# Output stores moved from ScalarE's DMA queue to SyncE's, and a small weight loaded between pieces of a larger one, in a retention and mixer kernel

## The chip, the cores and the metric

One core of one Trainium2 chip at a time. Times are microseconds (us) of device time for one execution. The profiler's span is the same execution without some 1.8 us at its start and end. A run counts as slow when it is more than 1.5% above the fastest of the same kernel, and else as fast. A ratio is the mean time of one kernel's fast runs over that of the kernel before, so it is not quite the ratio of the medians quoted; its 95% interval stands in brackets. The clock of a run is the mean share of its full clock that TensorE was granted.

## The reference, cut to what matters

```python
# q, k, v: (4 batches, 8 heads, 768 positions, 64)
state = gamma * state + k_t v_t^T ;  y_t = scale * q_t state      # retention
x = y as (4, 768, 512)
h  = x^T @ U @ V                  # U: 768 x 32, V: 32 x 768
u  = x + h^T
out = u + relu(u @ w_ch1) @ w_ch2 # 512 -> 2048 -> 512
```

The kernel calls u @ w_ch1 the up products and the second product the down products. It turns u by transposing DMAs (tile uT) before the up products of batches 2 and 3.

## The kernel before: the parts concerned

All loads are issued by SyncE (SP) in the order of a list. U and V go as one entry, ahead of w1:

```python
if key[0] == "uv":
    nc.sync.dma_start(out=Uf..., in_=moe_U...)
    for c in range(NCB):                       # NCB = 4
        nc.sync.dma_start(out=Vf[ds(RK * c, RK)], in_=moe_V)
    return
...
feed.append((("uv",), None))
for mb in range(4):
    for c in range(NCB):
        feed.append((("w1", mb, c), moe_w_ch1[ts(c, P), ts(mb, 512)]))
...
def prep_w1(mb):                               # GpSimd casts w1
    for c in range(NCB):
        nc.gpsimd.tensor_copy(out=w1b[:, c, ts(mb, 512)], in_=take("w1", mb, c))
        feed_one()                             # and the next load is issued
...
def hold_v():                                  # ScalarE casts V
    nc.scalar.activation(V4, Vf, AF.Copy)
```

A finished row block of the output (128 x 512, 256 KB) is put on a list of stores, with the engine that will issue it, and the turn of u is three transposing DMAs, of two row blocks each:

```python
def lr_turn(b, j):                             # j = 0 and 2; the third call is j = 4
    nc.sync.dma_start_transpose(
        out=uTs[b][:, ds(j, 2)]..., in_=us[b][:, ds(j, 2)]...)
...
elif r[1] == 2:
    stores.append((nc.sync if b > 1 else nc.scalar, out[b, ts(j, P)], r[0]))
```

So batch 1's six stores are issued by ScalarE, in the same microseconds in which SP issues batch 2's transposes.

Of the kernel before, what the change touches and what calls it, by code (L numbers as in the profile page):

```python
# [18 lines left out]
def kernel(  # L19
# [11 lines left out]
    nc = tc.nc  # L31
# [73 lines left out]
    feed = []  # L105
# [3 lines left out]
    def pair(b, sc):  # L109
        i = 2 * sc  # L110
        qs = [("q", b, sc, hh) for hh in range(2)]
        if b == 1:
            return [("k", b, i), *qs, ("v", b, i), ("k", b, i + 1),
                    ("v", b, i + 1)]
        return [("k", b, i), ("k", b, i + 1), *qs, ("v", b, i),
                ("v", b, i + 1)]

    def feed_keys(keys):
        for nm, b, i, *hh in keys:
            if nm == "q":  # L120
                src = q[b, ds(4 * hh[0], 4), ts(i, SC), :].rearrange(
                    "h (p two) d -> p h (two d)", two=2)
            else:
                src = (k if nm == "k" else v)[b, :, ts(i, P), :].rearrange(
                    "h p d -> p h d")
            feed.append(((nm, b, i, *hh), src))
# [8 lines left out]
    def feed_one(hold=True):  # L135
        if n_fed[0] == len(feed):
            return
        if hold and feed[n_fed[0]][0][:2] == ("k", 3):
            return
        key, src = feed[n_fed[0]]  # L140
        n_fed[0] += 1
        if key[0] == "uv":
            nc.sync.dma_start(
                out=Uf.rearrange("p s two r -> p s (two r)"),
                in_=moe_U.rearrange("(s p two) r -> p s (two r)", p=P, two=2))
            for c in range(NCB):
                nc.sync.dma_start(out=Vf[ds(RK * c, RK)], in_=moe_V)
            return
        t = rin.tile([P, 512], fp32, tag="in", name=f"in_{n_fed[0]}")
        ready[key] = t  # L150
        if key[0] in "qkv":
            t = t.rearrange("p (h d) -> p h d", h=H if len(key) == 3 else 4)
        nc.sync.dma_start(out=t, in_=src)  # L153

    def take(*key):
        assert feed[n_used[0]][0] == key, (feed[n_used[0]][0], key)
        n_used[0] += 1
        return ready.pop(key, None)
# [4 lines left out]
    for mb in range(4):  # L163
        for c in range(NCB):
            feed.append((("w1", mb, c), moe_w_ch1[ts(c, P), ts(mb, 512)]))
    feed_keys(pair(1, 0)[:AHEAD])
    for m in range(NM):
        feed.append((("w2", m), moe_w_ch2[ts(m, P)]))
# [3 lines left out]
    for _ in range(RING):  # L172
        feed_one()
# [79 lines left out]
    def prep_block(eng, nm, sc, hh):  # L253
        if hh == 0:
            pre[nm, sc] = blk.tile([P, 2, H, D], bf16, tag=nm + "0",
                                name=f"{nm}0_{sc}")
        t = pre[nm, sc][:, :, ds(4 * hh, 4)]
        src = take(nm, 0, sc, hh).rearrange("p (h two d) -> p two h d", h=4,
                                            two=2)
        if nm == "v":  # L260
            if eng == "A":
                nc.scalar.activation(t, src, AF.Copy)
            else:
                (nc.vector if eng == "D" else nc.gpsimd).tensor_copy(out=t,
                                                                     in_=src)
        else:
            g = (gq0 if nm == "q" else gk0)[:, sc, :, ds(4 * hh, 4), None]
            (nc.gpsimd if eng == "P" else nc.vector).tensor_tensor(
                t, src, g.to_broadcast([P, 2, 4, D]), op=ALU.mult)
        feed_one()  # L270

    def prep_keys(b, keys):
        for key in keys:
            nm, _, i, *hh = key
            src = take(*key)
            sc = i if nm == "q" else i // 2
            if nm == "q":
                if not hh[0]:
                    pre["q", b, i] = rpre.tile([P, 2, H, D], bf16, tag="qd",
                                               bufs=3, name=f"qd_{b}_{i}")  # L280
                t = pre["q", b, i][:, :, ds(4 * hh[0], 4)]
                src = src.rearrange("p (h two d) -> p two h d", h=4, two=2)
                g = gq0[:, i, :, ds(4 * hh[0], 4), None].to_broadcast(
                    [P, 2, 4, D])
            else:
                src = src.rearrange("p (h d) -> p h d", h=H)
            if nm == "k":
                if i % 2 == 0:
                    pre["k", b, sc] = rpre.tile([P, 2, H, D], bf16, tag="kd",
                                                bufs=3, name=f"kd_{b}_{sc}")  # L290
                t = pre["k", b, sc][:, i % 2]
                g = gk[:, i, :, None].to_broadcast([P, H, D])
            if nm == "v":
                t = rpre.tile([P, H, D], bf16, tag="vd", name=f"vd_{b}_{i}")
                pre["v", b, i] = t
                nc.gpsimd.tensor_copy(out=t, in_=src)  # L296
            else:
                nc.gpsimd.tensor_tensor(t, src, g, op=ALU.mult)  # L298
            feed_one()
# [23 lines left out]
    def prep_w1(mb):  # L323
        for c in range(NCB):
            nc.gpsimd.tensor_copy(out=w1b[:, c, ts(mb, 512)],  # L325
                                  in_=take("w1", mb, c))
            feed_one()

    def prep_w2(j):
        for m in range(4 * j, 4 * j + 4):  # L330
            nc.gpsimd.tensor_copy(out=w2b[:, m], in_=take("w2", m))  # L331
            feed_one()
# [3 lines left out]
    live = {}  # L336
# [245 lines left out]
             tp.rearrange("p (n t) -> p n t", t=P))  # L582

    def lr_turn(b, j):
        nc.sync.dma_start_transpose(
            out=uTs[b][:, ds(j, 2)].rearrange("p j c t -> p (j c) t"),
            in_=us[b][:, ds(j, 2)].rearrange("p j m -> p (j m)"))
# [7 lines left out]
    stores = []  # L595
# [32 lines left out]
    def down_pairs(b, gT, gS):  # L628
# [15 lines left out]
        def row(j):  # L644
            if j not in rows:
                rows[j] = [outp.tile([P, DM], fp32, tag="o_sb",
                                     name=f"o_{b}_{j}"), 0]
            return rows[j]
# [10 lines left out]
        def give(key, i, j, h, more):  # L659
            r = row(j)  # L660
            nc.vector.tensor_tensor(r[0][:, ds(DQ * h, DQ)], acc[key, i], more,
                                    op=ALU.add)
            r[1] += 1
            if end and i + 1 == NP:
                stores.append((nc.sync, out[b, ts(j, P), ds(DQ * h, DQ)],
                               r[0][:, ds(DQ * h, DQ)]))
            elif r[1] == 2:
                stores.append((nc.sync if b > 1 else nc.scalar,
                               out[b, ts(j, P)], r[0]))

        def p1(i):
# [3 lines left out]
        def p2(i):  # L675
            product("B", i, a12, w21, True)
            give("B", i, i, 0, held["a", i])
# [7 lines left out]
        def c22(i, nm):  # L685
            done.add((nm, i))
            if ("p5", i) in done and ("p7", i) in done:
                give("C", i, i + NP, 1, held["c", i])
# [32 lines left out]
        def p4(i):  # L721
            product("A", i, a22, t4, False)
            give("A", i, i + NP, 0, us[b][:, i + NP, :DQ])
# [175 lines left out]
    for mb in range(4):  # L899
        prep_w1(mb)  # L900
# [19 lines left out]
    for b in range(1, B + 1):  # L920
        tracks = []
        if b > 1:
            old = b - 1 < SEVEN
            first = [part(lr_expand, b - 1, 4, 2, "qk" if old else "st"),
                     part(lr_turn_pe, b - 1, 4, "qk" if old else "o")
                     if b < 3 else part(lr_turn, b - 1, 4)]
            if not old:
                RINGS["mlp"] = [6, 0, 1, 2]
# [131 lines left out]
```

## Time and profile before

| before | value |
|---|---|
| time, median of 3 runs | 221.32 us (221.21 to 221.44) |
| span of the profiled run | 220.5 us (its time was 222.3, 1 us above the median) |
| TensorE busy | 210.1 us |
| TensorE's wait for uT at 132.17 us | 1.95 us |

Two more lines of the page of the kernel before: the bytes of ScalarE's queue (packets, MB, share of 16 engines' span), and the costliest group of matmuls, whose last column is TensorE's idle time just before them and what ended most of it.

```profile
q10 hardware_dynamic: 1008, 1.64, 2.4%
...
L748 PE MATMUL mlp<-uT,w1b 128*128 128x512 f16 (+1 forms) x512 | 88.4, 326 | 2.5 <-DMA uT<-x 1.9
```

Of the 2.5 us that TensorE stood before all 512 up products, 1.9 are the one wait for the turned u. q10 is small over the whole span.

### The profile page before, as it was taken

What the parts mean: (1) busy time and instruction counts of PE and PEld (TensorE: products, weight loads), DVE (VectorE), ACT (ScalarE), POOL (GpSimd) and SP (SyncE); (2) the same over time, 40 slices, a digit from 0 to 9 for tenths busy, and PEclk for the clock granted to TensorE, in tenths of its full rate; (3) what the DMA queues carried; (4) which work ended last, traced back from release to release, by engine and by line L of the source; (5) the groups of instructions that cost most, each with busy time, mean ns of one, the idle gap of its engine ahead of it and who ended that gap; (6) DMA issues with size and microseconds to landing.
All of it is one profiled execution on the core that took longest, in us unless ns stands there. A gap on an engine that the chain in (4) does not pass through costs nothing.

```text
span 220.5 us, 5496 instructions
## 1 busy us (share of the span) xinstructions
PE 210.1 (95%) x2224; PEld 146.2 (66%) x2224; DVE 145.8 (66%) x300; ACT 92.9 (42%) x191; POOL 82.8 (38%) x119
## 2 busy tenths in 40 slices
PE   6879989999899999999999969999999999999994
PEld 2568744485555554656888854757788856668884
DVE  6478656233989539799686762598986443867443
ACT  3347664466446335667712005867510035551000
POOL 5466658998896869100089900000000000000000
PEclk9999999999999999999999999999999999999999
DMA  5999899999999999999999999600006340000043
GB/s 161 302 293 245 252 330 300 321 393 263 235 241 231 235 210 234 172 312 255 209 245 227 197 243 185 73 1 3 0 3 156 119 139 17 0 4 0 18 152 119
DMA packets 84569, 39.12 MB, mean 177 GB/s; under 512 B 58432, under 2 KB 77504, under 8 KB 84544
## 3 DMA queue, kind: packets, MB, share of 16 engines
q1 hardware_dynamic: 83536, 37.14, 72.0%
q10 hardware_dynamic: 1008, 1.64, 2.4%
q8 instruction: 17, 0.28, 0.6%
q14 instruction: 8, 0.07, 0.1%
HBM read 27.75 MB, written 6.29 MB: 154 GB/s over the span
## 4 chain that ended last, share of the span: by engine, by line
PE 69%; DMA 19%; DVE 3%; ACT 3%; POOL 2%; SPq 2%; issue 1%; DVEq 0%; ACTq 0%
PE mlp L748 28%; PE A L640 13%; DMA in<-in_moe_w_ch_dram 7%; PE mlp L799 7%; DMA in<-in_k_dram 6%; PE C L640 4%; DMA uT<-x 3%; PE B L640 3%; DMA in<-in_q_dram 2%; PE o L530 2%; ACT qT L85 2%; PE o L525 1%; PE s L491 1%; PE mlp L191 1%; SPq L153 1%
## 5 line engine op out<-in xcount | busy, mean ns | idle before, releaser
L748 PE MATMUL mlp<-uT,w1b 128*128 128x512 f16 (+1 forms) x512 | 88.4, 326 | 2.5 <-DMA uT<-x 1.9
L758 ACT ACTIVATE gT<-mlp 128x512 f16<-128x512 f32 (+1 forms) x98 | 47.3, 490 | 64.7 <-PE mlp L748 63.1
L748 PEld LDWEIGHTS <-w1b 128*128 128x128 f16 x512 | 48.2, 98 | 32.8 <-issue 2.1
L756 DVE TENSOR_SCALAR gT<-mlp 128x512 f16<-128x512 f32 (+1 forms) x30 | 16.6, 555 | 27.7 <-PE mlp L748 26.7
L640 PEld LDWEIGHTS <-gT 128*128 128x128 f16 x288 | 27.7, 98 | 3.3
L799 PE MATMUL mlp<-w2b,gT 128*128 128x512 f16 x96 | 23.7, 380 | 0.0
L298 POOL TENSOR_TENSOR kd<-in,gk 128x512 bf16<-128x512 f32 x18 | 19.2, 1082 | 4.6 <-DMA in<-in_k_dram 3.9
L640 PEld LDWEIGHTS <-gS 128*128 128x128 f16 x200 | 19.2, 98 | 2.6
L298 POOL TENSOR_TENSOR qd<-in,gq 128x512 bf16<-128x512 f32 x18 | 19.5, 1104 | 0.0
L640 PE MATMUL A<-w2t,gT 128*128 128x256 f16 x144 | 18.4, 273 | 0.0
L85 ACT ACTIVATE state<-st 64x256 bf16<-64x256 f32 x40 | 15.0, 374 | 6.7 <-PE st L371 3.8
L85 ACT ACTIVATE x<-o 128x512 f16<-128x512 f32 x20 | 11.9, 596 | 13.6 <-PE o L530 13.3
L501 DVE TENSOR_TENSOR a<-s,mask 128x512 bf16<-128x512 f32 x24 | 15.3, 680 | 2.4 <-PE s L491 2.4
L799 PEld LDWEIGHTS <-gT 128*128 128x128 f16 x96 | 8.4, 98 | 7.7 <-issue 0.2
L296 POOL CAST vd<-in 128x512 bf16<-128x512 f32 x18 | 11.2, 632 | 2.6 <-DMA in<-in_v_dram 2.4
L325 POOL CAST w1b<-in 128x512 f16<-128x512 f32 x16 | 9.7, 613 | 4.0 <-DMA in<-in_moe_w_ch_dram 3.4
L331 POOL CAST w2b<-in 128x512 f16<-128x512 f32 x16 | 10.0, 627 | 0.8
L640 PE MATMUL B<-w2b,gT 128*128 128x256 f16 x72 | 9.3, 273 | 0.0
L640 PE MATMUL A<-w2t,gS 128*128 128x256 f16 x72 | 9.0, 273 | 0.0
L640 PE MATMUL A<-w2b,gT 128*128 128x256 f16 x72 | 8.8, 273 | 0.0
L567 DVE TENSOR_TENSOR x<-s,x 128x256 f16<-128x256 f32 (+1 forms) x16 | 8.1, 548 | 0.6 <-PE qk L561 0.5
L593 POOL COPY gate<-gT 128x1 f16<-128x1 f16 x1 | 0.2, 190 | 21.9 <-DVE gT L593 21.9
(148 smaller groups left out, 292.2 us busy)
## 6 DMA issues: line engine op xcount, KB each, us to landing
in<-in_moe_w_ch_dram SPq DMA_DIRECT2D x32, 256.0 KB, 5.2
in<-in_k_dram SPq DMA_DIRECT2D x24, 256.0 KB, 5.5
in<-in_q_dram SPq DMA_DIRECT2D x24, 256.0 KB, 4.7
in<-in_v_dram SPq DMA_DIRECT2D x24, 256.0 KB, 5.3
out_dram<-o SPq DMA_DIRECT2D x16, 256.0 KB, 2.2
out_dram<-o ACTq DMA_DIRECT2D x6, 256.0 KB, 4.2
Vf<-in_moe_V_dram SPq DMA_DIRECT2D x4, 96.0 KB, 5.4
out_dram<-o SPq DMA_DIRECT2D x3, 128.0 KB, 1.7
```

The source lines that it names most:

```text
L85: nc.scalar.activation(dst, src, AF.Copy)
L296: nc.gpsimd.tensor_copy(out=t, in_=src)
L298: nc.gpsimd.tensor_tensor(t, src, g, op=ALU.mult)
L325: nc.gpsimd.tensor_copy(out=w1b[:, c, ts(mb, 512)], in_=take("w1", mb, c))
L331: nc.gpsimd.tensor_copy(out=w2b[:, m], in_=take("w2", m))
L501: nc.vector.tensor_tensor(a, four(sp[i]), causal(mask), op=ALU.mult)
L567: nc.vector.tensor_tensor(us[b][:, ds(j0, nj), ts(c, P)], four(grown[b][c])[:, :nj], xs[b][:, ds(j0, nj), ts(c, P)], op=ALU.add)
L640: nc.tensor.matmul(acc[key, i], lhs[:, m, ts(i, P)], rhs[:, m], start=(fresh and m == 0), stop=(m == NH - 1), skip_group_check=True)
L748: nc.tensor.matmul(g_p[:, :sz], w1b[:, c, ts(m, P)], uTs[b][:, ds(j, nj), c], start=(c == 0), stop=(c == NCB - 1))
L756: nc.vector.tensor_relu(gT[:, m, ds(lo, sz)], g_p[:, :sz])
L758: nc.scalar.activation(gT[:, m, ds(lo, sz)], g_p[:, :sz], AF.Relu)
L799: nc.tensor.matmul(ch, gT[:, m, ts(j, P)], w2b[:, m], start=(m == 0), stop=(m == NM - 1))
```

## The change

Its intent: let the transposes of batch 2's u go without company, with the stores behind them in the same queue, and let the first pieces of w1 arrive before V, which is needed later.

```diff
-            for c in range(NCB):
+            return
+        if key[0] == "v4":
+            for c in range(NCB):
                 nc.sync.dma_start(out=Vf[ds(RK * c, RK)], in_=moe_V)
             return
@@ the list of loads
             feed.append((("w1", mb, c), moe_w_ch1[ts(c, P), ts(mb, 512)]))
+            if mb == 0 and c == 1:
+                feed.append((("v4",), None))
@@ prep_w1, behind the second piece
+            if mb == 0 and c == 1:
+                take("v4")
+                feed_one()
@@ lr_turn
+        live["uT", b] = True
@@ the stores
-                stores.append((nc.sync if b > 1 else nc.scalar,
+                stores.append((nc.sync if b > 1 or ("uT", 2) in live else nc.scalar,
```

The first two of the six stores are recorded before the transposes and stay on ScalarE; four move.

## The prediction

> **What bounds the kernel now.** I read the page's slices first, then the chain of waits, then the timelines of TensorE, ScalarE's queue and the DMA engines around the one hole that they show. TensorE is busy for 210.1 of 220.5 us and its clock is granted in full, so a change can only win time where TensorE stands still, and both parts of this change move DMAs, not work.
>
> ```profile
> PE 210.1 (95%) x2224; PEld 146.2 (66%) x2224; DVE 145.8 (66%) x300; ACT 92.9 (42%) x191; POOL 82.8 (38%) x119
> PE   6879989999899999999999969999999999999994
> DMA  5999899999999999999999999600006340000043
> ```
>
> A slice is 5.5 us. After the first five slices there is one real hole in the PE row, the 6 in slice 24 (126.8 to 132.3 us). The chain of waits (start, us, what) shows what stands in it, and the timeline of TensorE and the view of the tile uT give it a size:
>
> ```profile
> 122.44 0.69 DVE x L567
> 123.27 1.28 SPq L585
> 124.64 7.39 DMA uT<-x
> 132.17 2.75 PE mlp L748 x12
> ...
> 178.30 20.91 PE mlp L748 x128
> ...
> 132.17 2.75 PE L748 MATMUL mlp<-uT,w1b 128*128 128x512 f16 x12 [1.95 <-DMA uT<-x]
> ...
> DMA to landing us min/median/max: 7.3/7.3/7.4
> ...
> DMA to landing us min/median/max: 3.0/3.2/3.2
> ```
>
> The reader is to see that TensorE waits 1.95 us for batch 2's turned u: two transposing DMAs of 256 KB, issued at 123.27 and 124.64, land after 7.3 and 7.4 us (first landing line), while the same DMAs for batch 3, at 166 to 180 us, take 3.0 to 3.2 us (second landing line) and leave no hole before 178.30. After 132.17 the chain is TensorE work alone, apart from gaps of 0.2 to 0.3 us, and it ends with the last output: what is won in the hole is won at the end.
>
> Why are they slow? ScalarE's queue stores batch 1's six outputs in the same microseconds, and the DMA engines' rate, in windows of 1 us, collapses:
>
> ```profile
> 120.43 10.40 ACTq L600 DMA_DIRECT2D out_dram<-o  x6
> ...
> 124.00:125.00 1.00, 1.00 (x11) 0.90 (x10) 0.55 (x2) 0.00 (x0) 1.00 (x3) 1.00 1.30 75
> 126.00:127.00 1.00, 1.00 (x12) 0.88 (x11) 0.51 (x2) 0.00 (x0) 1.00 (x3) 1.00 2.08 89
> 127.00:128.00 1.00, 1.00 (x12) 0.90 (x10) 0.42 (x1) 0.00 (x0) 0.13 (x1) 1.00 0.60 105
> 133.00:134.00 1.00, 1.00 (x6) 0.49 (x5) 0.00 (x0) 0.60 (x1) 0.00 (x0) 1.00 1.03 200
> 140.00:141.00 1.00, 1.00 (x16) 0.83 (x15) 0.19 (x1) 0.89 (x2) 0.00 (x0) 1.00 0.03 3
> ...
> q1 hardware_dynamic: 1626, 0.40, 60.2%
> q10 hardware_dynamic: 458, 0.84, 57.7%
> ```
>
> The last number of a window is GB/s. With transposes alone in flight (133 us) it is 200; with stores among them 75 to 105. But 140 to 141 us, with no store in flight, shows 3 GB/s: there, as just before 126 us, the DMA view shows one 16 KB packet of the "instruction" kind, after which the transposes' packets stand for about 1.4 us. So not all of the collapse is the stores' doing. The last two lines are the DMA view of 127.6 to 132.1 us, after that stall: SP's queue (q1) still moved 0.40 MB of transposes, ScalarE's (q10) 0.84 MB of stores.
>
> **What the Trainium skill says.** Page "DMA: Bandwidth & Descriptors", section "Queues, rings and completion order": SP and ACT each own one ring on each of the same 16 engines, every engine takes turns between rings by packet, and within a ring descriptors are consumed in order. The trace agrees: q1 and q10 both move throughout. It means that a store on ACT's queue takes turns with transposes that were issued before it and so stretches them, and that a store behind them in SP's queue does not. The same page, "Latency and other measured facts", gives a transposing DMA 261 GB/s; this trace has 181 to 200, and I use the trace. "Rules for kernel authors" says that spreading DMAs over queues saves issue time and gives no bandwidth; here ScalarE's issues are 0.34 us each and it has nothing to do then (its next ReLU waits for TensorE), so that saving is worth nothing.
>
> **The change part by part.** Part one, the stores. The order of instructions of the two programs differs little: of batch 1's six stores the first two stay on ACT (they are recorded before the u transposes), the other four leave ACT and stand in SP's order behind the first two u transposes and ahead of the third. TensorE's, VectorE's and GpSimd's orders do not change.
>
> What the transposes gain: until 127.6 us I leave things as they are, since stores one and two (issued at 120.43 and 121.95) still share the engines and the stall after the 16 KB packet has no store to blame. From there 0.40 MB at 200 GB/s take 2.0 us in place of the 3.4 or so seen, so the last packet passes at 129.6. An undisturbed transpose shows 3.2 us from issue to landing, of which 1.3 us are its 256 KB at 200 GB/s; from the DMA view of 166 to 169 us its first packet comes 1.2 us after the issue, which leaves 0.7 us behind the last packet. Landing: 129.6 + 0.7 = 130.3 us, against 132.03 (124.64 + 7.39) before. TensorE's last work before the hole is the eight-wide group of low-rank products that ends near 130.2 us, so it restarts near 130.4 in place of 132.17: 1.7 us won of at most 1.95.
>
> What the stores' new place could cost: stores three and four are ready when SP comes to them at about 127.6 (the end of the second transpose's issue); five and six wait for VectorE's sums, done at 129.58 and 130.45; the third u transpose waits for VectorE's last low-rank sum at 131.78 in any case, and a store's issue is 0.33 us. So the third goes out at 131.84 as before, lands near 135, and its first user, the first 256-wide product, is at 140.84 now and near 139.1 then: 4 us of slack. The output buffers are next written near 160 us. Cost: 0.
>
> Part two, V. In SP's order U, V x4, w1, w1, w1 becomes U, w1, w1, V x4, w1: from the third piece of w1 on, queue position, bytes ahead and semaphores are the same. The first two pieces land some 1.3 us earlier (393 KB of V at about 300 GB/s), V as much later. GpSimd and ScalarE, by their timelines:
>
> ```profile
> 23.20 1.15 POOL L403 TENSOR_TENSOR a<-a_raw,mask 128x512 bf16<-128x512 bf16 x1 [0.42 <-ACT a_raw L85]
> 24.30 1.16 POOL L325 CAST w1b<-in 128x512 f16<-128x512 f32 x2
> 26.08 0.61 POOL L325 CAST w1b<-in 128x512 f16<-128x512 f32 x1 [0.62 <-DMA in<-in_moe_w_ch_dram]
> 26.49 0.83 ACT L321 ACTIVATE V<-Vf 128x768 f16<-128x768 f32 x1
> ```
>
> GpSimd casts the first two pieces straight after its mask product, without a wait: earlier data starts nothing earlier. The wait that exists, 0.62 us, is for the third piece, which does not move. V landed at about 23.7 and would land near 25.0; ScalarE comes to it at 26.49, so 1.5 us of slack are left. Part two: 0, give or take 0.2 us.
>
> Sum: 221.32 - 1.7 + 0 = 219.6; I put it at 219.7, because the margin of the second landing over TensorE's free time is gone and small delays show at once.
>
> **The rivals.** (a) The stalls belong to the transposes and the instruction packets, the stores hardly matter. For it: 140 us. Then the landing comes down by a few tenths of a us and the time is 220.8 to 221.3. Against it: 3.4 us for 0.40 MB after the stall, with 0.84 MB of stores beside it. (b) The stores on ACT also cause the slow stretch from 123 to 125 us, when store three is issued (123.81). Then the landing falls to 129.5 or less, the hole closes entirely and the time is 219.2 to 219.4; TensorE's own end at 130.2 is then the bound, as before batch 3. (c) The third transpose, now behind four stores in one ordered queue, arrives late and opens a hole at the 256-wide products: 222 or more. The 4 us of slack speak against it. (d) V late: TensorE would wait for ScalarE's cast at 27 us, up to +1 us; it needs 1.5 us more delay than I find. (e) The early pieces of w1 do win something at the front: TensorE has a wait of 0.56 us at 59.33 behind the loads of batch 1, so at most that, 219.1.
>
> **Range and chances.** (a) to (b) span 219.2 to 221.2; I give my own sum and (b) together about four fifths, (a) 15%, (c) and (d) 5%. With 0.1 us of scatter between runs: 219.1 to 220.9. A gain of 2% would be 4.4 us, over twice the hole, and no path to it is visible; 2% slower needs a new wait of 4.4 us.
>
> **What would show it.** In the changed kernel's trace: four stores in SP's timeline between the second and third uT transposes; the first two uT transposes landing after 5.5 to 6 us; TensorE's wait for uT at most 0.5 us; the third transpose still issued near 131.8; GpSimd's first w1 casts at 24.3 and ScalarE's cast of V at 26.5, unmoved. I am wrong if the wait stays above 1 us, if a new wait stands at the 256-wide products, or if anything before 60 us moves by more than 0.3 us.

## The result and the profile after

| | before | after |
|---|---|---|
| time, median of 4 runs | 221.26 us (220.73 to 221.44) | 219.77 us (219.57 to 220.37) |
| span of the profiled run | 220.5 | 218.0 |
| first uT transpose, issued to landed | 123.27 to 130.53 | 122.74 to 128.00 |
| second uT transpose | 124.64 to 132.03 | 125.22 to 128.87 |
| up products of batch 2 start | 132.17 | 129.62 |

The ratio is 0.9941 [0.9915, 0.9967]: a gain of 0.6%, inside 2%.

The page of the changed kernel, in the lines that answer to those of before: the slices of TensorE, the bytes of ScalarE's queue, and the group of the up products.

```profile
PE   7879989999899999999999999999999999999994
...
q10 hardware_dynamic: 432, 0.59, 1.6%
...
L756 PE MATMUL mlp<-uT,w1b 128*128 128x512 f16 (+1 forms) x512 | 88.5, 326 | 0.6 <-ACT uT L85 0.6
```

The 6 in slice 24 is a 9 now, the releaser "DMA uT" is gone from the up products, and 1.05 MB have left q10. The timeline of SP's queue (start us, length us, what) shows where they went:

```profile
122.74 4.24 SPq L593 DMA_TRANSPOSE uT<-x  x2
127.08 3.21 SPq L608 DMA_DIRECT2D out_dram<-o  x4
131.31 1.24 SPq L593 DMA_TRANSPOSE uT<-x  x1
```

Four stores stand between the second and the third transpose. The view of the tile uT from 122 to 126 us gives the landings of the first two, and TensorE's timeline shows what stands ahead of the up products:

```profile
DMA to landing us min/median/max: 3.7/4.5/5.3
```

```profile
129.47 0.21 PE L568 MATMUL st<-pc,V 32*128 32x128 f16 x1
129.62 2.76 PE L756 MATMUL mlp<-uT,w1b 128*128 128x512 f16 x12
```

The up products follow the low-rank products with no wait in brackets. The rate of the DMA engines after the stall behind the instruction packet, in windows of 1 us (the last number is GB/s), is that of a queue of transposes with hardly anything beside it:

```profile
126.00:127.00 1.00, 1.00 (x11) 0.90 (x10) 0.55 (x2) 0.00 (x0) 0.60 (x2) 1.00 1.27 277
127.00:128.00 1.00, 1.00 (x12) 0.89 (x10) 0.55 (x2) 0.00 (x0) 0.00 (x0) 1.00 1.28 287
```

Before, the same two windows had 89 and 105 GB/s, but the stall behind that profile's own packet (126.2 to 127.6 us) falls into them, so they don't measure the stores. The fair pair is what came after each stall: 0.40 MB of transposes in 3.4 us, or 118 GB/s, beside the stores, against these 277 to 287. That looks like a closed case. It isn't quite: the two profiled spans differ by 2.53 us, the medians by 1.49, and the hole was 1.95. So the halves were tried alone, and both kernels again, in three later calls of runs, on the chips that the record numbers 1 and 4.

### The profile page after: what moved, and what is told of

It reads as the page before. It is cut to its first block, busy times and chain, and to the rows that moved or that the text cites. A ratio compares the mean times of both kernels' runs of the same rounds, so it can differ in the third digit from the quotient of the medians.

```text
span 218.0 us, 5496 instructions
## 1 busy us (share of the span) xinstructions
PE 210.3 (96%) x2224; PEld 146.6 (67%) x2224; DVE 144.8 (66%) x300; ACT 92.9 (43%) x191; POOL 82.0 (38%) x119
## 4 chain that ended last, share of the span: by engine, by line
PE 76%; DMA 15%; ACT 3%; POOL 2%; DVE 1%; SPq 1%; issue 1%; ACTq 0%
PE mlp L756 28%; PE A L648 15%; DMA in<-in_moe_w_ch_dram 7%; PE mlp L807 7%; PE C L648 6%; DMA in<-in_k_dram 6%; PE B L648 4%; DMA in<-in_q_dram 2%; PE o L537 2%; ACT qT L85 2%; PE o L532 1%; PE s L498 1%; PE mlp L195 1%; PE st L482 1%; POOL qd L302 1%; PE mlp L355 1%
## 5 line engine op out<-in xcount | busy, mean ns | idle before, releaser
L764 DVE TENSOR_SCALAR gT<-mlp 128x512 f16<-128x512 f32 (+1 forms) x30 | 16.7, 556 | 25.4 <-PE mlp L756 24.4
L812 DVE TENSOR_TENSOR o<-mlp,x 128x512 f32<-128x512 f32 x6 | 4.1, 688 | 6.5 <-PE mlp L807 6.5
```

The lines of the kernel that those rows point to most:

```text
L764: nc.vector.tensor_relu(gT[:, m, ds(lo, sz)], g_p[:, :sz])
```

## The experiments

Theory: stores on ScalarE's queue that run among the transposes stretch them until TensorE waits; V's place is worth nothing. Rivals: the queue and not the order is what counts; the instruction packet alone makes the hole; V's place gains or costs something.

Two measures are used for all profiles. One cuts the span at four points of TensorE's timeline: A, start to the first down product of batch 0; B, to the first up product of batch 1; C, to the first up product of batch 2 (the hole would be in it); D, to the end. The other is the time from the issue of the first uT transpose of batch 2 to the landing of the second. In all profiles without a hole but that of the doubled stores on SP, TensorE is free for the up products 6.88 us after that issue, so a landing beyond 6.88 is a hole. The last column is the start of one packet in the trace.

| profile | stores 3 to 6 | V | A | B | C | D | second uT landed, us after the first's issue | waits of 0.25 us or more at 58 to 61 us | "instruction" packet near 52 us, us after the first down product |
|---|---|---|---|---|---|---|---|---|---|
| before | ScalarE | old | 50.43 | 32.07 | 49.67 | 88.35 | 8.76 | 0.56 | 2.08 |
| e3 | ScalarE | old | 49.78 | 32.00 | 47.65 | 88.37 | 6.59 | 0 | 1.98 |
| e2 | ScalarE | moved | 49.59 | 34.33 | 47.65 | 88.39 | 6.50 | 2.66 | 4.47 |
| e9 | ScalarE | moved | 50.59 | 32.08 | 47.65 | 88.38 | 6.09 | 0 | 1.66 |
| e6 | ScalarE, doubled | old | 49.68 | 32.63 | 50.76 | 88.34 | 9.95 | 0.90 | 2.50 |
| e5 (slow) | ScalarE, late | old | 50.27 | 31.97 | 47.65 | 95.00 | 5.17 | 0 | 1.87 |
| after | SP | moved | 49.77 | 32.20 | 47.65 | 88.37 | 6.13 | 0.67 | 2.43 |
| e4 | SP | moved | 49.89 | 34.92 | 47.65 | 88.38 | 4.56 | 1.59 | 3.23 |
| e11 | SP | moved | 50.54 | 31.51 | 47.65 | 88.40 | 6.22 | 0 | 0.94 |
| e1 | SP | old | 50.49 | 32.08 | 47.65 | 88.38 | 5.29 | 0 | 1.86 |
| e10 | SP | old | 49.84 | 34.92 | 47.65 | 88.37 | 4.79 | 1.59 | 2.84 |
| e7 | SP, doubled | moved | 49.79 | 32.65 | 47.65 | 88.55 | 5.58 | 0.90 | 2.90 |
| e8 | SP | behind 4 | 50.47 | 33.59 | 47.65 | 88.37 | 5.27 | 1.92 | 3.33 |
| e12 | SP, all six | old | 50.34 | 33.27 | 47.65 | 88.38 | 5.88 | 1.59 | 2.84 |

C is 47.65 us in twelve of fourteen profiles, to the hundredth; it is 2.02 longer in the profile of the kernel before and 3.11 longer with the stores doubled on ScalarE. D is the same too. All other differences between spans but that of e5 are in A and B, before batch 1's up products, 35 us and more ahead of the stores.

One number sorts much of the scatter: the clock of each run. In the traces of e4 and e10 TensorE's clock stands at half for 3.41 us, from 61.32 and 61.20 us, and both runs have a mean clock of 0.992. Of the 83 runs 16 have a clock of 0.985 to 0.992, and their median is 223.2 us; the other 67 have 0.998 to 1.000, and theirs is 220.5. They are spread over kernels with the stores on either queue. Ten of the 16 still count as fast and stand in the ratios below.

### First call, one chip: the halves alone, and both kernels again

On this chip the kernel before had a median of 220.2 us (218.99 to 223.12, 11 runs).

**e1, the stores alone.** The diff is the two last hunks of the change.

> Only the stores are moved; V stays behind U. My theory (the gain is the hole at batch 2's turned u, V gives nothing): 1.2 to 2.0 us faster than before, TensorE's wait for uT under 0.3 us, second uT landing after 3.5 to 6 us, nothing new before 60 us. Rival (part of the gain is V's, at the front): 0.8 us or less faster, although the hole is closed in its trace.

Measured: 220.34 us median (219.95 to 223.19), ratio 1.0019 [0.9965, 1.0073]. The mechanism came as expected (no hole), the time didn't: 1.2 to 2.0 us were expected.

**e2, V alone.** The diff is the other hunks.

> Only V is moved. My theory: within 0.3 us of before, the wait of about 2 us for uT stays, and U's landing (22.4 us before, 21.0 us in the changed kernel) is run to run scatter. Rival (V directly behind U slows U's landing, TensorE's first low-rank product waits for it): 0.4 to 0.6 us faster than before, U landing near 21 us, the first products of w1 0.5 us earlier.

Measured: 221.1 us median (220.0 to 222.93), ratio 1.0035 [0.9981, 1.009]. In its profile the stores stand on ScalarE's queue, and yet there is no hole: the second transpose landed 6.50 us after the first's issue. So the wait that was to stay did not. It does have 2.66 us of waits near 60 us.

**e3, the kernel before again.**

> The kernel before, unchanged, as a second profile and a zero: ratio 1.000 within 0.002. If U's landing and the wait for uT scatter from run to run, this trace shows other numbers than 22.4 and 1.95 us; if they are fixed, within 0.2 us of these.

Measured: 221.32 us median (219.58 to 225.58), ratio 1.0033 [0.9969, 1.0097] to the other runs of the same kernel, where 1.000 within 0.002 was expected. This run changed the question. Its profile is of its fastest run, and it has no hole, with every store on ScalarE. The view of uT (122 to 127 us) and TensorE's timeline:

```profile
DMA to landing us min/median/max: 3.8/4.8/5.8
```

```profile
129.43 2.76 PE L748 MATMUL mlp<-uT,w1b 128*128 128x512 f16 x12
```

The second transpose landed 0.3 us before TensorE came to it. So the hole of the first profile belongs to the kernel before in some executions, not in each.

**e4, the whole change again.**

> The changed kernel once more, on this chip, as a second profile: 1.3 to 1.7 us faster than before (ratio 0.9925 to 0.994), hole closed, U landing near 21.0 us if the front gain is real, anywhere between 21 and 22.4 if it is scatter. The gains of stores alone and V alone should add up to this one within 0.4 us.

Measured: 220.9 us median (219.75 to 222.98), ratio 1.004 [0.9982, 1.0098]. No hole, but waits of 1.59 us near 60 us. On this chip nothing can be told apart: the intervals reach about a microsecond to each side, and all four contain 1. With runs at full clock alone, the 19 with the stores on ScalarE (the kernel before, e2, e3) average 220.6 us and the nine with them on SP (e1, e4) 220.3: 0.3 us, with a standard error as large.

### Second call, another chip: the order or the queue

Here the kernel before had 221.41 us (220.43 to 222.45, 7 runs).

**e5, all six stores stay on ScalarE but come after the transposes.** The list of stores is carried over into the next stretch of pieces and let out one by one.

```diff
-    def weave(keep, pieces, *tracks):
+    def weave(keep, pieces, *tracks, last=True, one=False):
...
-            for _ in range(0 if keep else late):
+            for _ in range(0 if keep else min(late, 1) if one else late):
                 store()
...
-        while stores:
+        while last and stores:
...
-        weave(b == 1, mlp_pieces(b - 1), *tracks)
+        weave(b <= 2, mlp_pieces(b - 1), *tracks, last=b != 2, one=b == 3)
```

> V where it was; all six stores of batch 1 stay on ScalarE's queue, but are issued one by one behind batch 2's first products, so after the first two u transposes. Theory (what hurts is that stores share the engines with the transposes in time, not which queue issues them): no wait for uT, both first transposes land 3.2 to 4.5 us after their issue but for one stall of about 1.4 us if an instruction packet falls on them; ScalarE's six issues of 0.34 us cost nothing TensorE sees. Rival (the queue itself, or its issues in front of ScalarE's ReLUs, matters): new waits of TensorE of over 0.5 us between 130 and 140 us.

Measured: 225.45 us median (222.26 to 226.67), two of four runs slow, ratio of the fast ones 1.0096 [1.0021, 1.017]. The two transposes landed 3.35 and 3.08 us after their issues, and no hole stands at uT. Order alone, on ScalarE's queue, thus came with an earlier second landing (5.17 us after the first's issue, against 6.1 to 8.8 with the stores among the transposes); that it closes the hole, one profile can't show, since three of those four had none either. But another hole opened. The profiled run is a slow one, so its length is not compared; the wait itself begins at 139.2 us, before its clock falls to half at 141.92. ScalarE's timeline and TensorE's:

```profile
140.96 0.34 ACTq L600 DMA_DIRECT2D out_dram<-o  x1
141.34 0.77 ACT L85 ACTIVATE state<-st 64x256 bf16<-64x256 f32 x2 [4.23 <-DMA kT<-kd]
```

```profile
142.78 1.86 PE L748 MATMUL mlp<-uT,w1b 128*128 128x256 f16 x8 [3.60 <-ACT gT L758]
```

In the trace the completions of all DMAs of both queues share eight semaphores in turn. The sixth late store got the one of a kT transpose that landed at 140.88, and went out at 140.96. Until then ScalarE, in order, stood for 4.23 us with that store at its head, could not carry the ReLU's results out of the accumulators, and TensorE waited 3.60 us. So the queue does matter, by way of the semaphore's wait and not of the issues' 0.34 us: the rival's band of 130 to 140 us has the start of this wait, but its cause wasn't foreseen. SP computes nothing that such a wait could hold up, ScalarE does.

**e6, the stores on ScalarE doubled.** Behind the second of the six stores, four more of 256 KB go to a spare tensor, on ScalarE.

```diff
+                n_act[0] += b == 1
+                if b == 1 and n_act[0] == 2:
+                    for i in range(4):
+                        stores.append((nc.scalar, spare_out[i],
+                                       w1b[:, i, ts(1, 1024)]))
```

> The kernel before, and four more stores of 256 KB from ScalarE's queue (weights to a scratch tensor) behind its second store. Theory: the suspected cost is doubled; another 1 MB in turns with the transposes, at 400 GB/s at best, puts the second uT landing 2.5 to 4 us further back, so the wait for uT is there in this run whatever the scatter, 2 to 5 us long, and the time is 1.5 to 4.5 us over before. Rival (stores do not matter, stalls by instruction packets make the hole): landing unchanged, wait 0 to 2 us, time as before within 0.7 us.

Measured: 223.02 us median (222.4 to 225.04), ratio 1.0095 [1.0039, 1.0151]. ScalarE's timeline and TensorE's:

```profile
122.20 3.67 ACTq L600 DMA_DIRECT2D spare_out<-w1b  x4
125.96 5.37 ACTq L600 DMA_DIRECT2D out_dram<-o  x4
```

```profile
133.07 2.76 PE L753 MATMUL mlp<-uT,w1b 128*128 128x512 f16 x12 [3.04 <-DMA uT<-x]
```

The transposes took 7.83 and 8.38 us, and the hole is 3.04 us. The second landed 3.4 to 3.9 us later, counted from the first's issue, than in the three profiles without a hole, and 1.2 later than in the one with it; 2.5 to 4 was expected.

**e7, the same four extra stores behind the transposes, on SP**, in the changed kernel (the same lines with nc.sync and n_act[0] == 3).

> The changed kernel, and the same four extra stores on SP's queue behind the second u transpose. Theory: in order behind the transposes they cost them nothing: both land as in the changed kernel, no wait for uT, time as the changed kernel within 0.5 us, so 2 to 5 us below the kernel with the extra stores on ScalarE's queue. Rival (any extra store traffic near the transposes costs): a wait for uT of over 1 us here too.

Measured: 220.86 us median (220.44 to 222.34), ratio 1.0004 [0.9952, 1.0056]. SP's timeline and TensorE's:

```profile
123.91 3.71 SPq L593 DMA_TRANSPOSE uT<-x  x2
127.67 2.03 SPq L608 DMA_DIRECT2D spare_out<-w1b  x4
```

```profile
130.09 2.76 PE L761 MATMUL mlp<-uT,w1b 128*128 128x512 f16 x12
```

The same megabyte costs over 2 us beside the transposes and nothing that these runs resolve behind them (at full clock alone, e6 averages 222.8 us in three runs and e7 220.7 in three). e6 and e7 are the pair that settles the direction: e6's interval lies above 1, and the profile puts the cost where the theory has it. They differ in queue, order and V's place at once; e5 changed the order alone, and e2 V's place. e7's third transpose landed at 136.71, later than the 134.53 of the changed kernel, and no wait stands at its first user, which starts at 138.12.

**e8, V behind four pieces of w1 in place of two**, in the changed kernel.

```diff
-            if mb == 0 and c == 1:
+            if mb == 0 and c == 3:
```

> The changed kernel with V behind four pieces of w1. Theory (TensorE's place before 59 us does not count, since the loads of batch 1 hold it there): V lands near 26.5, ScalarE's cast of V comes 0.5 to 0.8 us late, the first up product starts near 28.6 to 28.9 in place of 28.0, and the wait for batch 1's q near 59 us shrinks by as much, so that from 62 us on the kernel is where it was. Rival (the front counts in full): first down product and batch 1's up products 0.5 to 0.8 us later than in the changed kernel, too.

Measured: 221.46 us median (220.02 to 221.98), ratio 0.9998 [0.9951, 1.0046]. Now V is late, and ScalarE's timeline and TensorE's say so:

```profile
26.75 0.84 ACT L325 ACTIVATE V<-Vf 128x768 f16<-128x768 f32 x1 [0.99 <-DMA Vf<-in_moe_V_dram]
```

```profile
27.65 0.39 PE L854 MATMUL mlp<-V,pc 32*128 32x512 f16 x3 [0.96 <-ACT V L325]
```

The first up product starts at 28.70 us, as the theory had it; yet this and part A (50.47) lie among those of the kernels with V unmoved. The front differs by as much from run to run. The waits near 60 us did not shrink as expected: they are 1.92 us.

### Third call, the same chip: is V's place a cost?

In the first eight experiments the profiles with V moved had the longer waits near 60 us and the longer part B. The theory was that moving V costs about a microsecond there. The last four experiments were spent on it, all in the same rounds. The kernel before stands at 221.32 us (220.43 to 222.45, 8 runs), but seven of these eight are the runs of the second call; the one of this call took 220.65 us. So the ratios of e9 to e12 compare across calls, and an interval below 1 doesn't show a gain here.

**e9, V alone again.**

> V moved, stores left on ACT, a second time, to tell scatter from an effect. Theory (moving V costs at the loads of batch 1): U lands near 20.7 us in place of 21.6 to 22.4 and TensorE's first up product starts 0.3 to 0.5 us earlier after the first scores, but the waits near 59 to 61 us (for the scaled q, k or v of batch 1) sum to 0.7 us or more, and batch 1's up products start at 82.9 us or later; ratio 1.000 to 1.004. Rival (scatter): the waits there and the 82.x us are as in the kernel before, and the ratio is 0.997 to 1.000. Either way the hole at batch 2's uT may or may not be there; if the hole is a matter of where an instruction packet falls, the landings are 5.5 to 7.5 us after the issue.

Measured: 220.63 us median (220.03 to 224.94), two of six runs slow, ratio 0.9956 [0.9917, 0.9994]. No wait of 0.25 us near 60 us, and again no hole with the stores on ScalarE (landing after 6.09 us). The theory predicted 0.7 us or more of waits: it falls. The ratio lies below the rival's band, too, but see above for what it is a ratio to.

**e10, the stores alone again.**

> Stores moved, V left in place, a second time. Theory: no wait for uT above 0.3 us, the two landings 3.5 to 5.3 us after the issue, waits near 59 to 61 us below 0.6 us in sum, batch 1's up products at 82.6 us or earlier, and a ratio 0.993 to 0.999, lower than that of V alone by 0.003 or more. Rival (V's move is free or a gain): this kernel and the whole change run alike within 0.002. Rival (hole rare on this chip): ratio 0.999 to 1.002 with no hole in either profile.

Measured: 220.98 us median (219.93 to 223.1), ratio 0.9999 [0.9937, 1.0062]. V is in its old place, and the waits that were to come from moving it are there. TensorE's timeline, and its windows (busy us, granted clock, DMA share, GB/s):

```profile
58.74 0.29 PE L450 MATMUL qk<-ident,qd 128*128 128x128 bf16 x2 [0.69 <-POOL qd L298]
59.93 0.51 PE L450 MATMUL qk<-ident,qd 128*128 128x128 bf16 x6 [0.90 <-POOL qd L298]
```

```profile
60.00:62.00 2.00, 2.00 (x19) 0.80 1.06 265
62.00:64.00 2.00, 2.00 (x9) 0.50 1.18 258
```

Besides the 1.59 us of waits, the granted clock is at half for the 3.41 us from 61.20, and part B is 34.92 us. The whole change in e4 shows the same waits, the same half clock and the same 34.92. e12 below has the same waits with a full clock, and a B of 33.27:

```profile
62.00:64.00 2.00, 2.00 (x27) 1.00 1.17 291
```

The difference of the two B, 1.65 us, is what 3.41 us at half clock would cost (an estimate from these traces: half of 3.41 is 1.7). Two of e10's six runs have such a clock, 0.992, the profiled one among them (222.56 and 223.10 us); the other four average 220.46.

**e11, the whole change a third time.**

> The whole change on the same chip and in the same rounds as its two halves. Theory (stores gain where the hole is present, V gives back at 59 to 61 us): ratio 0.994 to 1.001, at or above the ratio of the stores alone; no hole at uT; waits near 59 to 61 us of 0.7 us or more in sum. Rival (the halves add up to a gain): below the ratio of the stores alone by 0.002 or more.

Measured: 220.29 us median (219.81 to 224.39), ratio 0.9955 [0.9922, 0.9988]; no hole, no wait at 60 us. V alone had 0.9956 and the stores alone 0.9999 in the same rounds. If these ratios are taken at face value V makes the gain. But the 0.9999 rests on e10's two runs at the lower clock: fast runs at full clock average 220.35 us in e9 (four), 220.46 in e10 (four) and 220.19 in e11 (five), which is no difference that these runs resolve. Nor do the profiles bear it out: with V moved, part A averages 50.03 us (e2, e4, e7, e9, e11 and after; e8 left out) and B 32.95; unmoved, 50.12 and 32.71 (seven profiles). The sums differ by 0.15 us, with a standard error of 0.6, and the three profiles of the whole change alone differ by 2.8.

**e12, all six stores on SP**, V in its old place: a candidate that also frees ScalarE's queue.

```diff
-                stores.append((nc.sync if b > 1 else nc.scalar,
+                stores.append((nc.sync,
```

> Candidate: V in its old place, and all six of batch 1's stores on SP's queue, so that the first two stand ahead of the u transposes in the same ordered queue. Theory: the transposes start behind 0.5 MB of stores at most, some 1.7 us at 290 GB/s, and since these stores are issued about 120 to 122 us and land before the first transpose is issued, nothing is lost: no hole at uT, ratio equal to that of the stores alone within 0.002. Rival (a store's wait holds SP's ordered queue): the first u transpose goes out later than 123.3 us, the second lands after 130 us, and the hole is back with 0.5 to 2 us, ratio 0.999 to 1.005.

Measured: 220.74 us median (219.74 to 221.48), ratio 0.9975 [0.9939, 1.0011]. SP's timeline:

```profile
122.94 1.02 SPq L600 DMA_DIRECT2D out_dram<-o  x2
124.39 4.03 SPq L585 DMA_TRANSPOSE uT<-x  x2
```

The first two stores went out behind the qT transpose and just ahead of the u transposes, not at 120 us as I had expected; the first landing took 4.70 us for it, and still no hole. It is as good as the changed kernel within the intervals (its six runs, all at full clock, average 220.72 us), and nothing tried is shown to beat it.

### What the experiments leave

Stores behind the transposes on SP: eight profiles, on two chips and in the result above, landings of 4.6 to 6.2 us, no hole. Stores on ScalarE among the transposes: landings of 6.1 to 8.8 us and one hole in four, and with twice the stores 9.95 us and a hole. The gain is a margin: a hole of 2 us comes in some executions of the one kernel, and in eight profiles of the other order it did not, with 0.60 us to spare at the least (e7; 0.66 in e11). One in four against none in eight could be chance; that the stores stretch the transposes rests on e6 and e7.

Why in some? The profiles suggest the "instruction" packet of 16 KB. Against the issue of the first u transpose it came 1.8 us later in the profile with the hole (125.1 us), and 0.5, 1.0 and 0.6 us later in e3, e2 and e9. With one hole among four this is a hint. These packets seem to belong to TensorE's own program: there are 17 of them for its 4448 matmuls and weight loads, and the one near 125 us starts between the 2731st and the 2771st of its some 4460 instructions in all fourteen profiles. And the profile with the hole had a second slow stretch, 75 GB/s from 124 to 125 us, ahead of its packet; what made that one, no run shows. How many of the unprofiled runs of the kernel before have the hole, and so what part of the 0.6% is the hole and what part the scatter of A and B, stays open: a run without a profile shows its time and its clock, but no wait.

The waits near 60 us rank almost without a fault with the time of another such packet (last column of the table): none up to 1.98 us after the first down product, 0.56 at 2.08, 2.66 at 4.47. Whether the packet makes the loads of batch 1 late, or both come late for another reason, no run shows. It is the same in kernels with V moved and unmoved. These waits and the stretches at half clock are the larger part of the scatter.

## Why the prediction was right

The number: 219.7 predicted, 219.77 measured, within the range of 219.1 to 220.9. That it fits to 0.1 us is luck, as the points show:

- **The stores stretch the transposes, and moved behind them they don't.** Right, and shown in both directions by e6 and e7. Rival (a), that the stores hardly matter, falls: the first two landings are 5.26 and 3.66 us after issue, with the stall of the instruction packet still there.
- **The size of that, 1.7 of at most 1.95 us.** The term that was mis-sized is the rate of transposes alone, taken as 200 GB/s from a window with single transposes in flight. With two in the queue it is 277 to 287. The second landed at 128.87 us where I had 130.3 (3.66 us after its issue, under the 5.5 to 6 that I had named as a sign), and the hole closed whole: C fell by 2.02 us. That is what rival (b) said of the hole, and with it (b) gave 219.2 to 219.4 us, not the 219.77 measured. Its cause, that the third store also makes the slow stretch of 123 to 125 us, isn't shown: the changed kernel has 6 GB/s from 124 to 125 us without that store, though behind a packet of its own at 123.58. Also, my windows were a selection: with stores among the transposes the kernel before also has 321 GB/s (125 to 126 us) and 400 (131 to 132), so the total rate doesn't show what the stores take; the transposes' own 118 GB/s do.
- **The place of the stores costs 0.** Right. The third transpose was issued at 131.31, landed at 134.53, and its first user starts at 137.64: 3.1 us of slack where I had 4. My reading was wrong by 0.66: the timeline merges products of both widths into one row, and the first 256-wide one of the kernel before starts at 140.18, not at 140.84. e7 left 1.4 us.
- **V's place: 0, give or take 0.2.** The net can't be told to 0.2 us: the means differ by 0.15, with a standard error of 0.6. Two steps of it were wrong. The slack of ScalarE's cast was to be 1.5 us; V landed at 25.4 and the cast began at 25.84, so 0.4 were left, and two pieces more of delay (e8) made a wait of 0.96 us. And my own sign of being wrong, that anything before 60 us moves by more than 0.3 us, came, as the timelines of GpSimd and of ScalarE in the changed kernel show:

```profile
24.14 1.17 POOL L329 CAST w1b<-in 128x512 f16<-128x512 f32 x2
```

```profile
25.84 0.83 ACT L325 ACTIVATE V<-Vf 128x768 f16<-128x768 f32 x1
```

The casts of w1 stayed, as predicted, but ScalarE's front came 0.65 us earlier and the first up product 0.66. U lands at 20.5 to 21.0 us in the seven profiles with V moved and at 21.0 to 22.4 in the seven others, so there seems to be an effect on U that I had not seen, perhaps because V's packets no longer follow right behind U's (argued, not tried). But the first up products start at 27.8 to 28.8 us in the one set and at 27.9 to 28.7 in the other, so it does not reach TensorE; e3, with V in its old place, has 28.01.
- **"What is won in the hole is won at the end."** Right: D is 88.34 to 88.40 us with and without the hole, in all but e5, whose other hole is in it, and e7 (its 0.2 us more were not looked into).
- **The step that failed without harm** is the first one, read as "there is one real hole" in the kernel before. It was in one profile; e3 shows the kernel without it. The scatter of 0.1 us between runs, taken from three close times, was also too small: later the two kernels run from 219 to 226 us, and e4 alone would have looked like no gain at all. The gain in the result's own rounds is clear of their noise, but how much of it the hole is stays open; that the medians differ by nearly the predicted amount is therefore partly luck.

## What to carry to other kernels

Here a DMA that TensorE waits for was delayed by stores on another queue (the second landing at 9.95 us in e6, at 5.58 in e7 with the same stores behind it). Try to put what nobody waits for behind it in the same queue, and to issue it from an engine that computes nothing: in e5 a store held ScalarE up until an older DMA had landed. Before sizing a gain, look at a second profile of the same kernel, and at the clock of every run: a hole that sits at the edge of a margin is there in one execution and gone in the next. Cutting the span at fixed points of the bound engine (A to D here) separates such a gain, here exact to 0.01 us, from scatter a hundred times as large elsewhere.

## What the Trainium skill lacked or had wrong

- "DMA: Bandwidth & Descriptors", "Rules for kernel authors", says that a transpose next to ordinary DMAs "needs nothing". The row is about keeping data correct, and they were in every run here; what it lacks is the time: two 256 KB transposes took 7.83 and 8.38 us with stores beside them and 4.36 and 3.12 with the same stores behind them.
- The same page, "Latency and other measured facts", gives a transposing DMA 261 GB/s with a non-contiguous middle dimension and some 350 to 400 for the contiguous case. Here single ones show 181 to 200 and two in a queue 277 to 287, so neither figure fits; that the number of them in flight could matter is not said.
- "Runtime: NRT & Kernel Launch", "Instruction fetch mechanics", has the 16 KB packets of the "instruction" kind, but neither it nor another page has the stall of transposes behind one: 6 GB/s in the microsecond from 124 to 125 us of the changed kernel, with three transposes in flight that land after 126 us.
- "TensorE: Matmul & The Clock Gate", "Part 1: The HAM clock gate", has the clock fall to half after an idle window of some 3.4 us. In e4 and e10 it fell to 0.5 although TensorE had been busy for 1.83 of the 3.41 us before (waits of 0.69 and 0.90 us with work between them); in e12, with waits of 0.70 and 0.89, and in e2, with 1.95 and 0.71, it did not. How much idle time in a window is enough is not said.
- "DMA: Bandwidth & Descriptors" puts a DMA's semaphore wait on the engine that issues it, but no page warns that a store issued from ScalarE can so hold up ScalarE's own work until an older DMA lands: 4.23 us in e5, and 3.60 us of TensorE's time.
